# A seven-tap convolution feeding a SwiGLU block: starting the next pair's convolution groups four, two and two chunks sooner

## The chip, the core and the metric

The kernel runs on one core of a Trainium2 chip. The metric is the device time of one execution in microseconds (us); of several runs the median is given. The core's engines work side by side, each through its own instructions in their order: TensorE (PE, with its weight loads listed as PEld), VectorE (DVE), ScalarE (ACT), GpSimd (POOL) and SyncE (SP). SP computes nothing here: it issues most DMAs and holds the waits that stand before them. An instruction waits for another engine by a semaphore.

## The reference

Inputs are `x` (8 x 4096 x 192), `weight` (8 heads x 7 taps) and three matrices of a feed-forward block. In float32:

```
w   = softmax(weight, axis=-1)                    # 8 heads, 7 taps
c[b, s, d] = sum_k w[d // 24, k] * x[b, s - 6 + k, d]   # zeros before each sequence
g   = c @ w_gate                                  # 192 -> 1536
out = (g * sigmoid(g) * (c @ w_val)) @ w_out      # 1536 -> 192
```

There are 32768 tokens. The kernel computes in float16 with float32 sums.

## The kernel before

**Tiling.** Tokens go in blocks of 512 (TB), two blocks to a *pair*, 32 pairs in all, four to a sequence. The 1536 inner features go in 12 *chunks* of 128. A block takes 12 steps, one chunk each, so a pair takes 24. In this document "chunk c of a pair" is a step from 0 to 23; chunks 0 to 11 serve the first block, 12 to 23 the second.

**One chunk on PE** (`Block.first`, L337 and L338): six matmuls of 512 columns, three into a `gate` bank and three into a `val` bank. They run on the lower and the upper 64 rows of the array at the same time. The 192 channels are cut into 128 (the "A" channels, one tensor per block: `xcA0`, `xcA1`) and 64 (the "B" channels of both blocks, stacked into one tensor `xcB`). Since gate takes its rows from the lower half and val from the upper half, each convolved tensor is needed a second time with its halves exchanged: `xsA`, `xsB`, made by two DMAs each in `Group.swap` (L311, L312). The second matmuls of chunk 0 already read `xsA` of A0.

ACT takes `silu` of the gate bank (L342) and DVE multiplies it by the val bank into `h` (L344). The second product (`piece`, L349) of the *previous* block runs in the same chunk, four steps of it, into `acc`, which has one buffer. ACT evacuates `acc` into `o` in chunks 5, 11, 17 and 23 (`evacuate`, L387), and SP stores it (L379). In those four chunks the pieces and the evacuation come before the chunk's first product, elsewhere behind it.

Two halves of the array write one bank of `acc`, one after the other. The later half must wait for the earlier; this passes through SP: `mark` (L229 to L234) puts a nop into SP's queue that waits for PE's piece, and PE's later piece waits for that nop. Marks stand in chunks 2, 8, 14 and 20, and PE waits for them in chunks 3, 9, 15 and 21. What SP has in its queue before a mark goes first, and what is behind waits for it.

**The convolution.** Pair 0 is convolved at the start. Each later pair p is convolved during pair p-1, in three *groups* B, A0, A1. A group's steps are
- `emit_x16`: once a pair, POOL issues DMAs that cast `x` to float16 in DRAM (`x16B`, `x16A`; L200 to L218),
- `load`: SP issues a transposing DMA into `xB` or `xA` (L250), six chunks before the group's start,
- `start_d` and two `act_tap`s: three products on ACT (L277, L281),
- two `dve_tap`s on DVE (L286),
- `pool_work`: two products (L294), three additions (L300) and the join (L304) on POOL,
- `swap`: the two DMAs above, on SP.

**What sets the order.** The program is written out by hand. `PLAN` gives each group a start `c`, counted in chunks from the start of the pair before its own, and each step an offset from it. They are entered in `todo` at an absolute chunk number and called when the loop over chunks has emitted that chunk's products, evacuation and store. So a number in `PLAN` decides the place of an instruction in its engine's queue; when it runs is left to the queue and its semaphores. Steps of the steady plan: `start_d` at +1, the products of ACT at +3 and +5, those of DVE at +2 and +4, POOL's work at +6, the swap at +13, the load at -6. The fetch stands at chunk 6 of the pair before that. Pair 1 has a plan of its own (`start1`, `swap1` and so on), which the change leaves alone.

```
at = base - 24 + PLAN["fetch1" if p == 2 else "fetch"]
todo.setdefault(at, []).append((emit_x16, p))
...
todo.setdefault(base + c - PLAN["lead"], []).append((Group.load, gr))
for o, f in steps + [(PLAN["swap" + alt][name], Group.swap)]:
    todo.setdefault(base + c + o, []).append((f, gr))
```

Here `base` is 24 * (p - 1), the first chunk of pair p - 1. Most tiles of the convolution have two buffers; the ones called `aD`, in a PSUM bank, have one.

Of the kernel before, what the change touches and what calls it, by code (L numbers as in the profile page):

```python
# [10 lines left out]


PLAN = dict(
    start={"B": 0, "A0": 7, "A1": 15}, swap={"B": 13, "A0": 13, "A1": 13},
    aD=1, aP=(3, 5), taps=(2, 4), pool=6, nact=2, npool=2,
    start1={"B": 3, "A0": 9, "A1": 16}, swap1={"B": 12, "A0": 12, "A1": 12},
    aD1=1, aP1=(3, 5), taps1=(2, 4), pool1=5, nact1=2, npool1=2,
# [552 lines left out]
```

## Time and profile before

| | |
|---|---|
| median of 3 runs | 787.63 us (787.38 to 788.08) |
| the profiled execution | 788.41 us |
| its span, first to last instruction | 786.7 us |
| granted TensorE clock, mean | 0.999 |
| PE busy | 769.5 us (98%) |
| POOL busy | 673.7 us (86%) |
| ACT busy | 654.5 us (83%) |
| DVE busy | 631.6 us (80%) |

The profile is taken from one execution. Busy time counts the engine's instructions, not their waits; PE's matmuls are pipelined, so 98% does not mean that PE runs at its peak. A row of the trace reads: start, duration, engine, line of the kernel, operation, output <- input, and, in brackets, the idle time before it with what ended it. SP's rows (SPq) are the issuing of a DMA; when its data has landed is given separately, from issue to landing. A row "A <- B: t, n, m" in the table of waits says that A waited for B for t us in n waits, the longest m. "<-issue" is time without a wait that the profile shows.

### The profile page before, as it was taken

The page shows a single profiled execution, that of the slowest core. Times are in us where ns is not written, and L with a number is a line of the kernel's source. Part 1 is how long each engine was busy: PE and PEld are TensorE (multiplying, and loading weights), DVE is VectorE, ACT ScalarE, POOL GpSimd, SP SyncE. Part 2 cuts the span into 40 slices and gives each one's busy share as a digit, 9 for nine tenths or more (in the row PEclk, how much of TensorE's full clock was granted, in tenths as well). Part 3 has the DMA queues.
Part 4 walks back from the last instruction along what each step waited for, and adds up shares of the span by engine and source line. Part 5 has one row for each costly group of instructions (what it writes and reads, how often), then busy time and mean ns, then how long its engine had stood idle before and what let it go on. Part 6 is the DMA issues. An engine that isn't in the chain of part 4 may idle for free.

```text
span 786.7 us, 27603 instructions
## 1 busy us (share of the span) xinstructions
PE 769.5 (98%) x10798; PEld 625.5 (80%) x10798; DVE 631.6 (80%) x980; ACT 654.5 (83%) x1193; POOL 673.7 (86%) x651
## 2 busy tenths in 40 slices
PE   7899999999999999999999999999999999999998
PEld 3588976897986897688798678978889779868976
DVE  7888887888887888788788888788888878887874
ACT  6888887888888888788888888888888888888874
POOL 7898899888899888898888898888998888998830
PEclk9999999999999999999999999999999999999999
DMA  9854455454465553454564554443557535554211
GB/s 139 112 89 69 89 93 93 80 87 76 86 94 94 83 85 73 90 88 83 86 82 84 87 98 83 83 77 86 93 89 88 86 74 89 93 90 84 69 46 52
DMA packets 172243, 67.25 MB, mean 85 GB/s; under 512 B 125136, under 2 KB 171728, under 8 KB 172112
## 3 DMA queue, kind: packets, MB, share of 16 engines
q1 hardware_dynamic: 103872, 51.71, 27.2%
q0 software_dynamic: 68240, 13.78, 22.0%
q8 instruction: 84, 1.38, 0.7%
q14 instruction: 47, 0.39, 0.2%
HBM read 29.13 MB, written 37.61 MB: 85 GB/s over the span
## 4 chain that ended last, share of the span: by engine, by line
PE 88%; DMA 6%; POOL 3%; issue 1%; ACT 1%; SPq 1%; DVE 0%; POOLq 0%
PE val L338 33%; PE acc L349 29%; PE gate L337 25%; DMA xsA<-xcA 6%; POOL t L300 1%; PE sumB L421 1%; SPq L311 1%; POOL t L294 1%; POOL xcA L304 0%; PE idle L145 0%; ACT silu L342 0%; DVE h L344 0%; ACT t L281 0%; POOL xcB L304 0%; POOL x16B L200 0%
## 5 line engine op out<-in xcount | busy, mean ns | idle before, releaser
L344 DVE TENSOR_TENSOR h<-silu,val 128x512 f16<-128x512 f16 x768 | 512.3, 685 | 143.2 <-ACT silu L342 114.7
L342 ACT ACTIVATE silu<-gate 128x512 f16<-128x512 f32 x768 | 448.5, 596 | 110.4 <-PE gate L337 81.3
L349 PE MATMUL acc<-wo_sb,h 64*128 64x192 f16 x6096 | 431.2, 243 | 0.2 <-DVE h L344 0.2
L349 PEld LDWEIGHTS <-h 64*128 64x128 f16 x6144 | 380.2, 94 | 58.1 <-DVE h L344 0.4
L300 POOL TENSOR_TENSOR t<-t,t 128x512 f32<-128x512 f32 x281 | 356.5, 1269 | 68.8 <-ACT t L281 51.1
L338 PE MATMUL val<-xsA,w_sb 64*128 64x512 f16 x768 | 288.7, 376 | 5.2 <-DMA xsA<-xcA 5.2
L337 PE MATMUL gate<-xcA,w_sb 64*128 64x512 f16 x768 | 288.5, 376 | 2.7 <-ACT silu L342 2.0
L337 PE MATMUL gate<-xsA,w_sb 64*128 64x512 f16 x768 | 288.6, 376 | 2.2 <-DMA xsA<-xcA 2.2
L338 PE MATMUL val<-xcA,w_sb 64*128 64x512 f16 x768 | 288.8, 376 | 0.4 <-DVE h L344 0.2
L338 PEld LDWEIGHTS <-w_sb 64*128 64x128 f16 x2304 | 207.8, 94 | 52.3 <-issue 8.4
L337 PEld LDWEIGHTS <-w_sb 64*128 64x128 f16 x2304 | 210.1, 94 | 38.6 <-issue 10.7
L337 PE MATMUL gate<-xcB,w_sb 64*128 64x512 f16 x384 | 144.5, 376 | 0.0
L338 PE MATMUL val<-xcB,w_sb 64*128 64x512 f16 x384 | 144.4, 376 | 0.0
L338 PE MATMUL val<-xsB,w_sb 64*128 64x512 f16 x384 | 144.3, 376 | 0.0
L337 PE MATMUL gate<-xsB,w_sb 64*128 64x512 f16 x384 | 144.3, 376 | 0.0
L294 POOL TENSOR_SCALAR t<-xA,wn 128x512 f32<-128x512 f16 x124 | 95.4, 873 | 0.2
L281 ACT ACTIVATE t<-xA,wn 128x512 f32<-128x512 f16 x124 | 89.0, 718 | 0.0
L304 POOL TENSOR_TENSOR xcA<-t,aS 128x512 f16<-128x512 f32 x62 | 78.6, 1268 | 4.9
L387 ACT COPY o<-acc 128x384 f32<-128x384 f32 x126 | 60.1, 477 | 8.2 <-PE acc L349 3.7
L286 DVE SCALAR_TENSOR_TENSOR aD<-xA,wn,aD 128x512 f32<-128x512 f16 x62 | 46.5, 749 | 0.0
L286 DVE SCALAR_TENSOR_TENSOR aS<-xA,wn,aD 128x512 f32<-128x512 f16 x62 | 46.0, 742 | 0.0
L281 ACT ACTIVATE t<-xB,wn 128x512 f32<-128x512 f16 x62 | 44.2, 713 | 0.0
(85 smaller groups left out, 327.9 us busy)
## 6 DMA issues: line engine op xcount, KB each, us to landing
out_dram<-o SPq DMA_DIRECT2D x128, 192.0 KB, 2.0
xsA<-xcA SPq DMA_DIRECT2D x126, 64.0 KB, 2.0
x16A<-in_x_dram POOLq DMA_DIRECT2D x24, 260.0 KB, 6.8
xsB<-xcB SPq DMA_DIRECT2D x62, 64.0 KB, 4.9
x16B<-in_x_dram POOLq DMA_DIRECT2D x24, 132.0 KB, 3.9
x16A<-in_x_dram POOLq DMA_DIRECT2D x7, 256.0 KB, 6.1
xA<-x16A SPq DMA_TRANSPOSE x62, 2.6
x_sb<-in_x_dram SPq DMA_DIRECT2D x2, 384.0 KB, 3.7
```

The source lines that it names most:

```text
L281: nc.scalar.mul(self.parts[-1], *self.tap(k, xt))
L286: nc.vector.scalar_tensor_tensor(out=to, in0=v, scalar=s, in1=self.aD, op0=ALU.mult, op1=ALU.add)
L294: nc.gpsimd.tensor_scalar(self.parts[-1], v, scalar1=s, scalar2=1.0, op0=ALU.mult, op1=ALU.mult)
L300: nc.gpsimd.tensor_tensor(self.parts[0], self.parts[0], t, op=ALU.add)
L304: ins = (eng or nc.gpsimd).tensor_tensor(xc, self.parts[0], self.aD, op=ALU.add)
L311: nc.sync.dma_start(out=sw[0:DB, :], in_=xc[DB:P, :])
L337: nc.tensor.matmul(g, w[0:DB, ca, f], a[0:DB, :], start=(i == 0), stop=(i == 2))
L338: nc.tensor.matmul(v, w[DB:P, cb, f], b[DB:P, :], start=(i == 0), stop=(i == 2))
L342: nc.scalar.activation(s, self.g.pop(j), AF.Silu)
L344: nc.vector.tensor_tensor(h, s, self.v.pop(j), op=ALU.mult)
L349: ins = nc.tensor.matmul(acc, self.h[j][r, ts(s, P)], wo_r[r, j, :], start=first and j == 0, stop=not first and j == NCH - 1, skip_group_c ...
L387: nc.scalar.copy(self.o[:, 2 * half : 2 * half + 2, :], self.acc[:, :, 0:D])
```

## The change

The steady plan's starts are lowered: B by four chunks, A0 and A1 by two. With the start, every step of the group moves by the same number, the load and the swap among them. The fetch at chunk 6 stays. A negative start places B's first steps in the pair before: `start_d` of B falls in chunk 21 there, DVE's first product in chunk 22 and ACT's in chunk 23, and its load in that pair's chunk 14. So while the groups A0 and A1 of one pair are still worked on, B of the pair after it, which lies two pairs ahead of the one that PE then computes, is begun.

| step (chunk of the pair p-1) | B before, after | A0 before, after | A1 before, after |
|---|---|---|---|
| load | -6, -10 | 1, -1 | 9, 7 |
| ACT: start_d, products | 1, 3, 5; -3, -1, 1 | 8, 10, 12; 6, 8, 10 | 16, 18, 20; 14, 16, 18 |
| DVE products | 2, 4; -2, 0 | 9, 11; 7, 9 | 17, 19; 15, 17 |
| POOL's work | 6, 2 | 13, 11 | 21, 19 |
| swap | 13, 9 | 20, 18 | 28, 26 |

```diff
 PLAN = dict(
-    start={"B": 0, "A0": 7, "A1": 15}, swap={"B": 13, "A0": 13, "A1": 13},
+    start={"B": -4, "A0": 5, "A1": 13}, swap={"B": 13, "A0": 13, "A1": 13},
     aD=1, aP=(3, 5), taps=(2, 4), pool=6, nact=2, npool=2,
```

## The prediction, made before the changed kernel was run

> **What bounds the kernel now.** I read the page first: busy shares, then the chain that ended last.
>
> ```profile
> span 786.7 us, 27603 instructions
> PE 769.5 (98%) x10798; PEld 625.5 (80%) x10798; DVE 631.6 (80%) x980; ACT 654.5 (83%) x1193; POOL 673.7 (86%) x651
> ...
> PE 88%; DMA 6%; POOL 3%; issue 1%; ACT 1%; SPq 1%; DVE 0%; POOLq 0%
> ```
>
> TensorE (PE) sets the end; the one thing beside it with a share worth having is a DMA. The table of PE's waits names it:
>
> ```profile
> PE val L338 <- DMA xsA<-xcA: 5.2, 8, 1.1
> ...
> PE gate L337 <- DMA xsA<-xcA: 2.2, 4, 0.8
> ```
>
> xsA is the half-swapped copy of an A group, made by two DMAs on SP's queue (L311, L312). To size the loss I took the start of the first gate matmul of every pair (24 chunks) from PE's rows. Seventeen of pairs 1 to 30 take 23.53 or 23.54 us. The other thirteen, less 23.53: pair 2 1.00, 5 1.25, 7 0.16, 10 0.97, 13 1.30, 15 0.69, 18 0.83, 19 0.04, 21 0.68, 22 0.25, 23 0.43, 26 0.66, 29 0.96. That is 9.2 us, all but 0.1 of it in chunk 0, which lasts 0.98 in an undisturbed pair; the last pair's chunk 0 lasts 1.34, 0.36 more. Together 9.6 us. The table's 7.4 is the part where a matmul is named; I use the 9.6, since the pairs really last that much longer.
>
> How it comes about, at the boundary of pairs 4 and 5. Pair 4 starts at 110.89, pair 5 at 134.43. First POOL, finishing A0 of the next pair, then SP's queue (start, duration), then PE:
>
> ```profile
> 118.30 1.27 POOL L300 TENSOR_TENSOR t<-t,t 128x512 f32<-128x512 f32 x1 [1.02 <-ACT t L281]
> ...
> 128.48 1.27 POOL L304 TENSOR_TENSOR xcA<-t,aS 128x512 f16<-128x512 f32 x1
> ```
>
> ```profile
> 129.02 0.38 SPq L379 DMA_DIRECT2D out_dram<-o  x1
> 129.50 1.16 SPq L250 DMA_TRANSPOSE xB<-x16B  x1
> 131.88 0.46 SPq L311 DMA_DIRECT2D xsA<-xcA  x1
> 132.39 0.62 SPq L312 DMA_DIRECT2D xsA<-xcA  x1
> ```
>
> ```profile
> 131.16 0.51 PE L349 MATMUL acc<-wo_sb,h 64*128 64x192 f16 x8
> ...
> 134.64 0.38 PE L337 MATMUL gate<-xsA,w_sb 64*128 64x512 f16 x1
> 136.09 0.37 PE L338 MATMUL val<-xsA,w_sb 64*128 64x512 f16 x1 [1.07 <-DMA xsA<-xcA]
> ```
>
> A0 is joined at 129.75, yet its swap leaves at 131.88, 2.13 us later. SP is not busy in between: after the load of xB it stands at the mark of chunk 20 (L232), which waits for that chunk's second-product matmuls, and these end at 131.67. The swap was emitted in chunk 20 too (7 + 13), behind the mark. So it leaves 20.98 us into the pair whatever POOL does. The second half leaves at 132.39, its row gives 3.7 us to landing, so it lands at 136.1. PE could have used it at about 134.8. Over all boundaries a landing up to 0.37 us into the pair costs nothing and each us beyond costs one: 0.38 gave 0.04, 0.62 gave 0.25, 0.81 gave 0.43, 1.05 gave 0.69, 1.66 gave 1.25 and 1.30. From that place the usual 2.0 us just suffices (landing 0.04 us before the pair starts), and any slower landing is paid. Those that the trace shows reach from 1.9 to 3.7 us.
>
> **The change, part by part.** It changes no instruction and no duration. PE's and POOL's orders stay as they are (POOL: B, the next fetch, A0, A1). What moves stands on SP, ACT and DVE.
>
> *SP.* Per pair the queue was: A1's swap (chunk 4), store 5, mark 8, A1's load (9), store 11, B's swap (13), mark 14, store 17, B's load (18), mark 20, A0's swap (20), store 23, A0's load (1 of the next). It becomes: A1's swap (2, behind mark 2), store 5, A1's load (7), mark 8, B's swap (9), store 11, mark 14, B's load (14), store 17, A0's swap (18), mark 20, store 23, A0's load (23). A0's swap passes mark 20 and B's load and stands straight behind store 17. In the rows above that store is issued at 129.40, and 0.1 later the queue is free, at 129.50; A0 joins at 129.75 where POOL stays as late as now. So the swap leaves at about 129.8, 18.9 into the pair and 2.1 us sooner, its second half at 130.3. With the slowest landing of this swap, 3.7, it is there at 134.0, against a need at 134.8. Every one of the fourteen stalls is covered: **minus 9.6 us**.
>
> What is now late behind it: mark 20 waits for the swap. The two issues end at about 130.9 in this pair, before chunk 20's matmuls end at 131.67, so PE's chunk 21, which waits for the mark, sees nothing. B's load moves to chunk 14 and needs x16B, which POOL fetches after B's join (10.0 into the pair) and which lands in 3.9: 13.9 to 14.9, where mark 14 lets the load go at about 15. Its bound is nothing or some tenths of SP time with nothing urgent behind it. A0's and A1's loads ask for x16A fetched a pair earlier. B's swap at 9 has fifteen chunks before its use; A1's leaves about where it does now. **0 us.**
>
> *POOL.* B's chain waits 0.40 and 1.02 us for ACT's two products in a typical pair (51.1 us over the run). With B's products four chunks sooner that wait goes, and POOL runs up to 1.4 us earlier with each pair, until the next late thing holds it: A1's second product, chunk 18 instead of 20. Three groups at 6.75 and 1.6 for the fetch are 22 us in a period of 23.53, so POOL has the room. PE wins nothing from this, but A0's join moves forward, by up to 4 or 5 us, and so the landing's margin grows.
>
> *ACT and DVE.* Their additions are the same ones, in other gaps between silu and h. DVE is 80% busy, and its products wait for ACT, not the reverse: 0. On ACT what matters is the evacuation of acc, since acc has one buffer and PE's next half waits for it:
>
> ```profile
> 408.74 0.71 ACT L281 ACTIVATE t<-xA,wn 128x512 f32<-128x512 f16 x1
> 409.35 0.47 ACT L387 COPY o<-acc 128x384 f32<-128x384 f32 x1
> ```
>
> Here a convolution product stands right before evacuation 11. The chunk behind such an evacuation lasts 1.01 to 1.02 in place of 0.98; that happens twice a pair now (11: product in chunk 10; 17: in chunk 16), and it will twice again (10 and 16). Evacuations 5 and 23 get the nearest product two or more chunks ahead, as 5 and 23 have now. **0 us**, between minus 2.2 (31 pairs times 2 times 0.035, if both vanish) and plus 1.5 (a further 0.05 a pair).
>
> *The seam.* Pair 1 keeps its own plan, so in pair 0 B of pair 2 meets A1 of pair 1: in chunk 21 ACT has two products in a row (0.71 and 0.69), and B's load holds SP until x16B, issued at 27.92 and 3.9 in flight, lands at 31.8; B's swap for pair 1 then goes at about 33.7 instead of 31.04, and at xsB's median of 4.9 its second half lands near 39.2, just before pair 1 starts at 39.3. Bound 0 to 1.5 us once; I take 0.2, since the slow edge needs the slowest xsB landing (6.5).
>
> *Sum.* 788.41 - 9.6 + 0.2 = 779.0 for an execution like the profiled one. That one is 0.78 above the median of 787.63, and the stalls hang on landings that vary; the others may just have had fewer. I shift by less than half of it and say **778.7**.
>
> **A rule to weigh.** xsB's swap, issued some 2 us behind the fetch of x16, has a median of 4.9 to landing where xsA's has 2.0, for the same 64 KB. The Trainium skill, "DMA: Bandwidth & Descriptors", section "Queues, rings and completion order", says that each DMA engine serves the queue rows with work in turn, packet by packet; the trace agrees as far as the 4.9 goes. The case it threatens is the second rival.
>
> **The rivals.** *Slower, by ACT.* Evacuations start 0.6 us behind acc's last matmul when a product stands before them, and that already shows as 0.03 to 0.04. If A0's three products (chunks 6, 8, 10), now following evacuation 5 closely, leave ACT a backlog at evacuation 11, each tenth more is paid in full. It decides from about 0.18 us at both evacuations: 2 x 0.18 x 31 = 11.2, more than the gain: 790. Against it: ACT idles 0.26 for PE before silu 10 in the same spacing today. Chance 0.06.
>
> *Contention.* POOL moves the fetch, and A0's swap moves towards it. If they met, 4.9 from a second half at 19.1 into the pair lands at 24.0, against 23.53 + 0.37 = 23.9: 0.1 a pair, 3 us back, 781.8. Against it: x16A lands 6.8 after an issue at 10.8, so by 17.6, and earlier once POOL gains. Chance 0.08.
>
> *It doesn't do what it says.* The landing follows something else at the boundary, so the stalls move along: 787.6. Against it, the 2.13 us in which A0 lay finished. Chance 0.04.
>
> **How the numbers follow.** My forecast has 0.82. The range reaches from 776.5 (both evacuation delays gone) to 782.5 (the seam's bound, or contention). A measurement of this kernel tells some 0.2% (1.6 us) from no change. Faster: 0.82 + 0.08 = 0.90; same 0.04; slower 0.06.
>
> **What would show it.** Right: A0's swap leaves 18 to 19 into the pair; no wait of PE on xsA; all pairs at 23.5; POOL's waits on ACT move from B to A1. Wrong: pairs over 23.6 with chunks 12 or 18 beyond 1.02 (ACT), chunk 21 waiting for the mark (A0 joined after 20), or xsA landings over 4.5.

## The result, and the profile after

The changed kernel takes 779.21 us (median of four runs, 777.58 to 779.74) against 787.50 for the kernel before beside it; the ratio is 0.9895 (95% interval 0.9872 to 0.9918). The profiled execution took 778.69 us, 9.72 less than that of before, and its span is 777.0. Measured once more on another chip, the ratio was 0.9867 (0.9845 to 0.9889).

The page's head, the busy line and the chain that ended last:

```profile
span 777.0 us, 27603 instructions
PE 768.0 (99%) x10798; PEld 529.2 (68%) x10798; DVE 631.6 (81%) x980; ACT 654.5 (84%) x1193; POOL 674.7 (87%) x651
...
PE 97%; DVE 1%; ACT 1%; issue 1%; POOL 0%; POOLq 0%; DVEq 0%
```

PE, DVE, ACT and POOL are busy as long as before, to within 1.5 us; the chain's 6% of DMA is gone. PEld's busy time fell from 625.5 to 529.2 us, with as many weight loads of the same mean length, so they overlap more; an undisturbed pair lasts 23.53 us with either. In the table of PE's waits (total, times, longest) no row names xsA any more. The largest rows left are these, and all but the second belong to the start of the program:

```profile
PE idle L145 <- DVE wmax L163: 2.5, 1, 2.5
PE gate L337 <- ACT silu L342: 0.9, 3, 0.4
PE gate L337 <- ACT xsB L441: 0.7, 1, 0.7
```

PE's weight loads have rows of their own, and this one has grown (0.3 us in one wait before):

```profile
PEld L349 <- SPq L232: 2.3, 6, 0.5
```

The same boundary as in the prediction, pairs 4 and 5, now at 109.53 and 133.06. POOL's fetch and its join of A0, then SP's queue:

```profile
116.67 1.31 POOL L200 DMA_DIRECT2D x16B<-in_x_dram  x1
...
124.29 1.27 POOL L304 TENSOR_TENSOR xcA<-t,aS 128x512 f16<-128x512 f32 x1
```

```profile
124.62 1.13 SPq L250 DMA_TRANSPOSE xB<-x16B  x1
127.66 0.38 SPq L379 DMA_DIRECT2D out_dram<-o  x1
128.13 0.47 SPq L311 DMA_DIRECT2D xsA<-xcA  x1
128.65 0.59 SPq L312 DMA_DIRECT2D xsA<-xcA  x1
```

B's load left three microseconds before store 17, and the swap stands right behind that store: 18.60 us into the pair, where it was 20.98. Its second half took 2.0 to land, at 130.7, and PE needs it at about 133.4. In this pair A0 was joined at 125.56, so the swap now waits for the store and no longer for a mark.

By the starts of the pairs' first matmuls, the 9.7 us of the span come from these places: the first chunks of pairs 2 to 31 lost less by 9.5, and chunk 21 of pair 18 by 0.1; pairs 1, 2, 8 and 22 got 0.26, 0.20, 0.24 and 0.03 longer; pair 0 has a chunk of 1.20 at its end (0.65 before, so 0.55 more). The rest, 1.4 less, is the program's start: pair 0 began 0.8 later, but its chunks 6 and 12 took 1.30 and 0.98 in place of 2.60 and 1.84. That part is not the change's: both chunks come before the first instruction that the change moves, B's load in chunk 14 of pair 0. Over the twelve profiles of this study pair 0 lasts between 21.94 and 24.29 us, whatever the plan, and the two profiles of the changed kernel alone differ by 0.25 there.

The new waits, those of the weight loads on L232, are for marks. In pair 8 a swap's issue took 2.17 us; then PE's weight load behind mark 20:

```profile
222.25 0.47 SPq L311 DMA_DIRECT2D xsA<-xcA  x1
222.76 2.17 SPq L312 DMA_DIRECT2D xsA<-xcA  x1
```

```profile
225.12 0.28 PEld L349 LDWEIGHTS <-h 64*128 64x128 f16 x8 [0.54 <-SPq L232]
```

The issue ended at 224.93, the mark followed, and PE's chunk 21 came 0.24 late.

### The profile page after: what moved, and what is told of

It is laid out like the page before. It is cut to its first block, busy times and chain, and to the rows that moved or that the text cites. A ratio compares the mean times of both kernels' runs of the same rounds, so it can differ in the third digit from the quotient of the medians.

```text
span 777.0 us, 27603 instructions
## 1 busy us (share of the span) xinstructions
PE 768.0 (99%) x10798; PEld 529.2 (68%) x10798; DVE 631.6 (81%) x980; ACT 654.5 (84%) x1193; POOL 674.7 (87%) x651
## 3 DMA queue, kind: packets, MB, share of 16 engines
q8 instruction: 84, 1.38, 0.8%
## 4 chain that ended last, share of the span: by engine, by line
PE 97%; DVE 1%; ACT 1%; issue 1%; POOL 0%; POOLq 0%; DVEq 0%
PE gate L337 55%; PE acc L349 32%; PE val L338 8%; PE sumB L421 1%; DVE h L344 1%; ACT silu L342 0%; PE idle L145 0%; PE xt L260 0%; DVE aS L286 0%; PE gate L349 0%; PE val L349 0%; PE wn_ps L174 0%; DVE aD L286 0%; ACT t L281 0%; ACT xcB L429 0%
## 5 line engine op out<-in xcount | busy, mean ns | idle before, releaser
L300 POOL TENSOR_TENSOR t<-t,t 128x512 f32<-128x512 f32 x281 | 357.2, 1271 | 57.6 <-ACT t L281 40.3
L349 PEld LDWEIGHTS <-h 64*128 64x128 f16 x6144 | 301.4, 94 | 123.2 <-SPq L232 2.3
L349 PE MATMUL acc<-wo_sb,h 64*128 64x192 f16 x6096 | 370.2, 243 | 0.5 <-DVE h L344 0.4
```

The source lines that it names most:

```text
L300: nc.gpsimd.tensor_tensor(self.parts[0], self.parts[0], t, op=ALU.add)
L349: ins = nc.tensor.matmul(acc, self.h[j][r, ts(s, P)], wo_r[r, j, :], start=first and j == 0, stop=not first and j == NCH - 1, skip_group_c ...
```

## The experiments

The theory: what is won is the place of A0's swap in SP's queue, ahead of mark 20. The rivals: the head start of B on POOL wins it; or the slow landings came from B's load, which stood 2.4 us ahead of the swap. Times are medians; the ratio is to the kernel before on the same chip. "Starts as before" is B 0, A0 7, A1 15; "as after" is B -4, A0 5, A1 13.

**e1: only the swap.** Starts as before.

```diff
-    swap={"B": 13, "A0": 13, "A1": 13},
+    swap={"B": 13, "A0": 11, "A1": 13},
```

> All starts as before; only A0's swap is entered two chunks sooner (chunk 18, ahead of mark 20 and of B's load). Theory (the swap's place in SP's queue is all that counts): the swap leaves when A0 is joined, about 18.9 us into the pair, lands by 23.2 even at 3.7 us, no wait on xsA is left, 778 to 779.5 us; POOL's waits on ACT stay near 51 us. Rival (the earlier start of the groups is what pays): nothing moves, 786 to 788 us.

Measured: 791.56 us, ratio 1.0066 (1.0053 to 1.0079): slower, which neither theory had. The wait on xsA is gone all the same (0.2 us in all). But PE's weight loads wait for marks, and chunk 21 lasts 1.23 to 2.5 in nearly every pair. The row of the waits, then SP's queue in the pair that began at 302.93, and PE's wait behind it:

```profile
PEld L349 <- SPq L232: 24.9, 32, 1.7
```

```profile
321.06 0.38 SPq L379 DMA_DIRECT2D out_dram<-o  x1
321.82 0.46 SPq L311 DMA_DIRECT2D xsA<-xcA  x1
322.34 0.59 SPq L312 DMA_DIRECT2D xsA<-xcA  x1
323.03 1.22 SPq L250 DMA_TRANSPOSE xB<-x16B  x1
```

```profile
324.43 0.28 PEld L349 LDWEIGHTS <-h 64*128 64x128 f16 x8 [0.56 <-SPq L232]
```

The swap waits for A0's join (321.80), and behind it, still ahead of mark 20, stands B's load of chunk 18. It ends at 324.25; only then does the mark pass. So the stall moved from the swap to the mark, and is paid in every pair: against 0.98 for an undisturbed chunk, chunk 21 of pairs 1 to 30 loses 14.9 us, where before chunk 0 lost 9.5.

**e2: the change without the swap's new place.** Starts as after, A0's swap in chunk 20.

```diff
-    start={"B": 0, "A0": 7, "A1": 15}, swap={"B": 13, "A0": 13, "A1": 13},
+    start={"B": -4, "A0": 5, "A1": 13}, swap={"B": 13, "A0": 15, "A1": 13},
```

> Starts as after; only A0's swap is put back to chunk 20, behind mark 20. Theory: it leaves 21.0 us into the pair although A0 is joined at about 14.6, about 13 boundaries stall again, 786 to 788 us. Rival 1 (the earlier start pays by itself): 778 to 780 us. Rival 2 (the slow landings come from B's load, whose transposing DMA stood 2.4 us ahead of the swap and is now at chunk 14): the swap still leaves at 21.0, but all landings are near 2.0 and nothing stalls, 778 to 780 us.

Measured: 786.44 us, ratio 0.9996 (0.9987 to 1.0004): no change, as the theory said, and both rivals fall. POOL runs ahead as in the changed kernel, B's load is out of the swap's way, and the waits of PE are back:

```profile
PE val L338 <- DMA xsA<-xcA: 5.6, 9, 1.3
PE gate L337 <- DMA xsA<-xcA: 1.2, 3, 0.6
```

**e3: only B sooner.** A0 and A1 as before.

```diff
-    start={"B": 0, "A0": 7, "A1": 15},
+    start={"B": -4, "A0": 7, "A1": 15},
```

> Only B starts four chunks sooner; A0 and A1 as before. Theory: A0's swap stays behind mark 20, stalls on xsA as before, and the chunk of 1.20 at the end of pair 0 is there: 786 to 788.5 us. Rival 1 (B's head start on POOL pays): 778 to 780 us. Rival 2 (B's load was what slowed the swap): 778 to 780 us.

Measured: 790.11 us, ratio 1.0046 (1.0031 to 1.0060). The stalls are there as in before (chunk 0 loses 8.3 us), so the rivals fall again; but it is slower than the theory's upper end. The profiled execution, the fastest of six (788.1), shows part of why. Chunk 18 of pair 1 lasts 2.74, 1.7 too much, once: A1's load took 6.35 us to land, ACT stood 1.61 for it, and the evacuation that PE needed stood behind. And chunk 1 lasts 1.02 to 1.03 in most pairs that don't stall. Where the slower executions spend the rest of the 3.6 us is not known.

**e4: only A0 and A1 sooner.** B as before.

```diff
-    start={"B": 0, "A0": 7, "A1": 15},
+    start={"B": 0, "A0": 5, "A1": 13},
```

> Only A0 and A1 start two chunks sooner; B as before. Theory: the whole gain, 778 to 779.5 us, with A0's swap leaving 18.9 us into the pair, POOL still waiting for ACT's products of B, and no chunk of 1.20 at the end of pair 0. Rival (B's head start is needed, else the swap comes too late): between 781 and 787 us.

Measured: 792.34 us, ratio 1.0068 (1.0053 to 1.0084): a miss of the same kind as e1. B's load is in chunk 18 between swap and mark 20; 21.8 us of the weight loads' waits for marks, and chunk 21 loses 12.3. So B's four chunks are needed after all. The question that e1 and e4 leave: for B's head start on POOL, or for the place of its load?

**e6: e1, and B's load in chunk 14.** Starts as before.

```diff
-    swap={"B": 13, "A0": 13, "A1": 13},
+    swap={"B": 13, "A0": 11, "A1": 13},
...
-    todo.setdefault(base + c - PLAN["lead"], []).append((Group.load, gr))
+    todo.setdefault(base + c - (10 if name == "B" else PLAN["lead"]), []).append((Group.load, gr))
```

> As e1 (starts as before, A0's swap in chunk 18), and B's load, which in e1 stood between that swap and mark 20, now in chunk 14. Theory: e1 lost because the load (1.2 us of issue behind a swap that leaves at 18.9) held mark 20; without it the swap's issue ends at 20.0 and the time is that of after or up to 1.5 us more for the swaps whose issue takes 2 us, 778 to 781 us, POOL's waits as before. Rival (B's head start on POOL is needed): 785 us or more.

Measured: 778.48 us, ratio 0.9865 (0.9846 to 0.9883): all that the change wins (0.9867 for the changed kernel on the same chip, after_again below), with every start where it was. POOL still waits 41.6 us for ACT and joins A0 18.9 us into the pair. The pair that began at 298.58:

```profile
313.67 1.13 SPq L250 DMA_TRANSPOSE xB<-x16B  x1
316.71 0.38 SPq L379 DMA_DIRECT2D out_dram<-o  x1
317.49 0.46 SPq L311 DMA_DIRECT2D xsA<-xcA  x1
318.00 0.59 SPq L312 DMA_DIRECT2D xsA<-xcA  x1
```

Now the issue ends at 318.59, 20.0 us into the pair, ahead of the matmuls that mark 20 waits for. Two entries of SP's queue give the whole gain; ACT's, DVE's and POOL's earlier work gives nothing by itself, as e2 showed.

**e5, e7, e8, e9: can more be had?** e5 asks what the 1.01 to 1.02 in chunks 12 and 18 are.

```diff
-    start={"B": 0, "A0": 7, "A1": 15},
+    start={"B": -4, "A0": 6, "A1": 12},
```

> As after, but A0 starts at 6 and A1 at 12, so that no product of ACT stands in chunks 10 and 16, right before an evacuation. If the 0.03 to 0.04 us in chunks 12 and 18 come from that, these become 0.98 and the kernel is some 2 us faster than after, 776 to 777.5 us. If they come from the silus behind the evacuation, they stay and so does the time, 778 to 779.5 us.

Measured: 780.74 us, ratio 0.9896 (0.9873 to 0.9918), no gain on the changed kernel and above both ranges. The reading of ACT was right: chunks 12 and 18 last 0.98, and an undisturbed pair 23.46. DVE's products moved along with ACT's, but it is the evacuation that shows it: by their medians, evacuations 11 and 17 start 0.04 us behind the end of acc's last matmul, and 0.46 behind it in the changed kernel. But A1's swap now stands in chunk 1 and A0's load in chunk 0, both ahead of mark 2, and a slow issue there is paid in chunk 3, 5.4 us over the run. In pair 16:

```profile
393.59 2.62 SPq L250 DMA_TRANSPOSE xA<-x16A  x1
396.31 0.54 SPq L311 DMA_DIRECT2D xsA<-xcA  x1
396.90 0.59 SPq L312 DMA_DIRECT2D xsA<-xcA  x1
```

e7 puts the changed kernel's swap ahead of store 17 (`"A0": 11`, starts as after).

> As after, but A0's swap in chunk 16, ahead of store 17. The swap leaves at about 16 us in steady pairs, so a slow issue of 2 us no longer reaches mark 20: the waits of PE for a mark in chunk 21 go, those in chunk 9 stay; 0.3 to 0.6 us less than after. If these waits don't come from the swap's issue, the time stays that of after.

Measured: 778.62 us, ratio 0.9867 (0.9849 to 0.9884). The waits in chunk 21 of the steady pairs are gone, and those in chunk 9 stay (1.06 in pair 2, 1.33 in pair 18), as expected, but the 0.3 to 0.6 us are not won: in pair 1 POOL joins A0 only 20.1 us in, the swap and then the held-back store 17 are issued from there to 59.51, 21.8 us in, mark 20 comes behind both, and chunk 21 lasts 1.75.

e8 joins both (`"A0": 6, "A1": 12`, A0's swap at +10) and starts B of pair 2 two chunks later.

> e5 and e7 together (A0 from 6, A1 from 12, A0's swap in chunk 16), and B of pair 2 two chunks later than in after, so that in pair 0 its first product doesn't meet the last of A1 in chunk 21. Besides what e5 and e7 give, the chunk of 1.20 at the end of pair 0 becomes 0.65: about 0.55 us less than both together, 775.5 to 777 us if both hold.

Measured: 780.71 us, ratio 0.9894 (0.9877 to 0.9910), so a miss. Pair 0 does end with 0.65, but mark 2 costs 2.6 us, mark 8 of pair 26 1.0, and pair 1 another 1.4: 0.9 in chunk 21 behind a mark, 0.5 in chunk 0, where PE waits for xsA.

e9 keeps the starts of e5 (B of pair 2 again two chunks later) and moves what stood ahead of marks.

```diff
-    start={"B": 0, "A0": 7, "A1": 15}, swap={"B": 13, "A0": 13, "A1": 13},
+    start={"B": -4, "A0": 6, "A1": 12}, swap={"B": 13, "A0": 10, "A1": 14},
...
-    todo.setdefault(base + c - PLAN["lead"], []).append((Group.load, gr))
-    for o, f in steps + [(PLAN["swap" + alt][name], Group.swap)]:
+    todo.setdefault(base + c - {"B": 6, "A0": 7, "A1": 4}[name], []).append((Group.load, gr))
+    later = 2 * (1 < p < 6 and name == "A0")
+    c += 2 * (p == 2 and name == "B")
+    for o, f in steps + [(PLAN["swap" + alt][name] + later, Group.swap)]:
```

> A0 from 6 and A1 from 12 as in e5, but no DMA of SP stands shortly ahead of a mark: A0's load in chunk 23 (7 ahead of its start), A1's in chunk 8 behind mark 8 (4 ahead), A1's swap in chunk 2 behind mark 2, A0's swap in chunk 16 (18 for pairs 2 to 5), B of pair 2 two chunks later with its load where after has it. Theory (the 0.035 us twice a pair come from ACT, and the rest of e5's and e8's loss from issues of 2 us that hold a mark): pairs of 23.46, hardly a wait on a mark, 2 to 3 us less than after. If the waits on marks stay, no better than after.

> The changed kernel itself, unchanged, beside e9 on the same chip: 0.985 to 0.991 of the kernel before; e9 lies below it by 0.3% if the theory holds.

Measured side by side: e9 776.85 us (776.06 to 778.20), ratio 0.9861 (0.9840 to 0.9882); the changed kernel (after_again) 777.58 (776.88 to 778.84). By their traces e9 is ahead: its pairs 1 to 30 take 705.5 us against 707.1 (706.6 in the changed kernel's first profile), all but three of them 23.46, and two waits for marks are left:

```profile
PEld L349 <- SPq L232: 0.7, 2, 0.4
```

But the 2 to 3 us that were expected did not come: the medians are 0.7 us apart and their ranges overlap. The traces are of one execution each, and the program's start alone varies by more than 0.7, so that e9 is faster is likely, not shown by the times.

## Why the prediction was right, point by point

**The stalls, minus 9.6.** Right, in cause and size. The swap was held by mark 20 (e2: put back behind the mark, all of the gain is gone), the slowest landing is covered from the new place, and chunk 0 lasts 0.97 to 1.00 in pairs 1 to 31. The slow landings are still there: of 54 with a record nine took 2.7 to 3.8 us (in before, fifteen of 54 took 2.5 to 3.7). They stopped mattering.

**SP's other entries, 0.** The outcome was right, the account wrong. I priced the move of B's load to chunk 14 at nothing and named no price for its cover. It was the cover: with the load left in chunk 18, e1 and e4 lose 14.9 and 12.3 us in chunk 21, more than the stalls that they remove. The prediction did write that mark 20 comes behind the swap and that PE's chunk 21 waits for it; it then worked out the end of the swap's issue alone, without asking what would stand there if B were left as it was. As a rival on the slower side this was a better one than ACT's evacuations. A second point of the same line: "PE's chunk 21 sees nothing" holds for issues of 0.47 and 0.59. Where an issue takes 2 us, the mark behind it is late: mark 20 in pair 8, and mark 8 in pair 2, there behind A1's load. So two of the signs that I had named for being wrong did appear, though small: pairs 1, 2 and 8 took 23.73 to 23.80, and in pairs 1 and 8 chunk 21 waited for its mark, in pair 1 with A0 joined after 20, as I had written, in pair 8 with A0 joined long before.

**POOL.** Right: A0's join moved from 18.85 to 14.65 into the pair within five pairs, B's wait shrank from 1.42 to 0.20, and A1 now waits about 0.55 and 0.70 for ACT's products. POOL's waits on ACT moved more than they shrank (51.1 us before, 40.3 now, 41.6 in e6 with no start moved). That it wins nothing for PE is shown by e6, which has none of it.

**ACT and DVE, 0.** Right: chunks 12 and 18 still last 1.01 to 1.02, an undisturbed pair still 23.53, and the rival by ACT's backlog didn't come about. The cause given for the 0.035 was right too (e5's evacuations).

**The seam, 0.2.** Mis-sized: 0.55 in pair 0 and 0.26 in pair 1, where POOL has not caught up yet, joins A0 20.2 us in, and mark 20 waits for the swap. The 0.8 is within the bound of 1.5. ACT's rows at the end of pair 0 (37.22 to 38.32 us), and then PE's weight load:

```profile
37.22 0.69 ACT L277 ACTIVATE aD<-xB,wn 128x512 f32<-128x512 f16 x1 [0.17 <-DVE aS L286]
37.84 0.58 ACT L342 ACTIVATE silu<-gate 128x512 f16<-128x512 f32 x1
```

```profile
38.47 0.09 PEld L337 LDWEIGHTS <-w_sb 64*128 64x128 f16 x1 [0.69 <-ACT silu L342]
```

What I missed is that aD has one buffer: B's first product had to wait for A1's last use of it on DVE, and the silu stood behind. In e1, e4, e8 and e9, which don't bring the two together in chunk 21, pair 0 ends with 0.65; in e2, e3 and e5, which do, with 1.20. Yet little of the 0.55 could have been saved. In those four the first chunk of pair 1 lasts 1.38 to 1.53 instead: PE waits for the xsA of pair 1, whose second half lands 0.8 to 0.9 into the pair, because POOL joins that A0 late. In the changed kernel it lands at 38.88; had pair 1 begun 0.55 sooner, at 37.93, the landing would have been 0.95 into the pair, and by the prediction's 0.37 about 0.6 late (an estimate). Only in before and e6, where pair 0 was long (24.29 and 23.54), does neither loss show. B's swap for pair 1, the other half of that bound, cost nothing: chunk 0 of pair 1 lasts 1.00.

**The sum.** 9.6 off and 1.3 on, for the seam and for marks that were priced at nothing, make 8.3, where the prediction had 9.4. The profiled execution fell by 9.7 because another 1.4 came off at the program's start, which is chance. The medians fell by 8.3 beside the first runs and by 10.4 beside those of after_again, so they don't decide between these. That the measured median lies within 0.5 of 778.7 is partly luck: the forecast was reckoned from an execution 0.8 above the median of before, less 0.3, and that offset covers about half of the 1.1 that the sum left out.

**Contention and the rule on queues.** A0's swap didn't meet the fetch: it is issued 18.6 into the pair and the fetch now goes 7.1 into the pair shown, 5.7 in later ones. The runs don't test the rule for that case.

## What to carry to other kernels

In a queue that carries both data and permissions, a DMA that waits delays every permission behind it: count, for each such mark, the issue times and the waits of all that stands ahead of it, and when one entry is moved past a mark, look at what else is left in between. An edit that is priced at nothing should be tried without, on paper at least; here a gain of 1.3% (e6) and a loss of 0.7% (e1) differ by the place of one load. A transfer whose usual landing just suffices is late whenever it isn't usual.

## What the runs showed of the hardware that was not expected

SP's DMA issues have usual lengths (0.47, 0.59, 1.15 us for L311, L312, L250), but some take up to 1.7, 2.2 and 2.8, and some swaps land in 2.5 to 3.8 us in place of 2. Both go with a packet of an instruction queue. The queues' lines around A0's swap in the changed kernel, first in pair 8 (221.8 to 226.0), then in pair 9 (245.1 to 249.3):

```profile
q1 hardware_dynamic: 427, 0.33, 28.7%
q8 instruction: 1, 0.02, 2.6%
```

```profile
q1 hardware_dynamic: 432, 0.33, 28.6%
```

Over four kernels (before, after, e2, e6) and 120 swaps of A0, counting from 1 us before the swap to 2.2 behind it: of 69 with a packet of queue 8 or 14 in that time 34 were slow (a landing of 2.5 us or more, or an issue over 0.8), of 51 without one 1 was. Counted in the same way over all twelve profiles, 109 of 207 swaps with such a packet were slow, and 1 of 153 without. All 21 issues of L250 over 1.4 us behind pair 0 in the four kernels had one too, between 1 us ahead of the issue and 0.3 behind its end. The slow swaps come in the same pairs again and again: 1, 4, 12, 14, 17, 20, 21, 22, 28 and 30 are slow in before and in e2 alike, which is why the stalls looked irregular and yet repeated. They also go by the time at which the swap leaves: 21.0 us into the pair, in before and e2, twelve and eleven swaps are slow; 18.6 to 18.9 into it, in both profiles of the changed kernel and in e6, it is the same six in all three (8, 11, 16, 19, 24, 27). That the packet is the cause, not a companion, was not tried.
